# Attention with a relative-position bias and two expert layers on one core: the loads of two head pairs, the order of the attention sums and the split of x are moved

## Chip, cores and metric

One core of one Trainium2 chip. The time is device microseconds of one execution of the whole program; less is better. A kernel's time is the median of several executions.

## What is computed

Four batches of 8 heads, 576 tokens, head width 64. The attention output, reshaped to 2304 tokens of 512 values, goes through a layer with a rational activation and then through a layer with a maximum of three products:

```
scores = q @ k.T / 8
x      = log1p(|i - j|) / log1p(max(i, 1))
bias   = relu(x * w1 + b1) @ w2               # hidden width 32, one value per head
attn   = softmax(scores + bias)
x      = attn @ v                             # as [2304, 512]
h      = x @ w_in                             # [2304, 2048]
x      = (P(h) / Q(h)) @ w_out                # P cubic in h, Q quadratic in |h|
out    = max(x @ w1, x @ w2, x @ w3) @ w_out  # hidden width 768
```

## The kernel before

All in one instruction stream per engine, in the order in which the Python code writes it: the schedule of SP (which issues every DMA), TensorE, VectorE, GpSimd and ScalarE is the program order, so an instruction that waits holds up all that stands behind it on its engine.

**Bias stage.** The bias is the same for all batches. 36 groups (`bgroups`: five row tiles `t` of 128 queries, the last one of 64, in groups `g` of 16 rows) are made one after another. `bias_hidden` (L181, L183) writes four tiles `h` per group, one on ScalarE and three on VectorE as a rule, two groups ahead. `bias_out` multiplies them (L192), scales the result on ScalarE into `bo` (L198), and SP stores it to DRAM (L200). Three groups after a row tile is complete, `bias_load` (L207) reads it back for the head pairs 0 and 1; this waits on SP until the tile's stores have landed. In the same loop VectorE splits k and q of pairs 0 and 1 into high and low parts. A list `L0` says ahead of which group k and q (`load_kq`, L128 and L130) and v (`load_v`, L122) of pairs 2 and 3 of batch 0 are issued.

Most SBUF tiles (`h`, `bo`, bias tiles, k, q and v of batch 0, their splits, exponentials) share 35 buffers with the tag `slot`. A buffer is taken from those that are free; when none is, the first instruction that writes the new tile waits.

**Attention.** 80 units (`units`): one row tile of one head pair. In batch 0 the first two pairs go row tile by row tile (10 units), where the sums are handled by unit (`own`). All other pairs go in two groups: row tiles 0 and 1 (a two-unit group), then 2, 3 and 4 (a three-unit group). `attn_tick(n)` walks a list of steps, `A2`; unit n has its scores (`sc`, L241) and, on VectorE, the addition of the bias with the running minimum (`r0`, `r1`, L267), then the exponentials on ScalarE (`e0`, `e1`, L273). Unit n-1 has its sums guarded on GpSimd (`na`, L298), and at the end of its group `sums_turn` (`n`) takes reciprocals (L313), transposes them and SP writes them to DRAM (L323); `sums_load` (L333) reads them back, broadcast, into `att`, two units later. Unit n-2 is transposed on TensorE (`T`, L369, L375) into PSUM banks (four of the tag `bank`), which `v0` and `v1` copy out. When a group is through, `attn_v` (`av`, L420) multiplies by v, in one piece for two units and in pieces for three; then `st` runs `attn_store` (L426): VectorE multiplies the product by the returned reciprocals into `xs`, and SP stores that to `x_d` a unit later (L428).

In `attn_tick`, `loads_at` and `splits_at` say at which unit k and q of a later pair are loaded and at which unit GpSimd starts to split them (the first such step is L141). A pair whose load was issued already is skipped there. For pair 3 of batch 0 these are units 8 and 11.

**Turn to the FFN.** Eight units before the end (72) the first block of x is read back (`load_x`, L560). In each of the last four units `split_x` makes one quarter: ScalarE copies it (L567), GpSimd subtracts (L568), VectorE for the last quarter. Then the FFN runs: `ph` and `y` (L576), with the rational function on ScalarE and VectorE (L607 to L623) and its split `gs` (L633, L634) in between. The first steps of the FFN are mixed with the last `attn_tick` calls, from unit 80 on.

Of the kernel before, what the change touches and what calls it, by code (L numbers as in the profile page):

```python
# [26 lines left out]
HID = 32  # L27
TOFF = 572
TW = 1148
KN = {'RL': 2, 'NSG': 4, 'RX': 2, 'AVL': 2, 'NSLOT': 35, 'NRAW': 3, 'NRAWX': 2, 'NATT': 4, 'HB': 0, 'NE': 'd', 'FP': 2, 'BL': 4, 'T4': 0, 'LSP': 1, 'KX': 4, 'HT': 'ss', 'EVP': 'da', 'TTP': 'dda', 'NXS': 4, 'EARLY': 4, 'NM0': 0, 'MAN': 3, 'MANF': 3, 'HA': 2, 'H0': [34, 35], 'L0': [(14, 'k2'), (18, 'v2'), (24, 'k3')], 'B4': 2, 'H2': [1, 2, 4, 6, 8, 10, 12, 14, 16], 'SP0': [3, 4], 'BW': 3, 'A2': ['na', 'sc', 'sq1', 'av', 'T', 'r0', 'r1', 'n', 'st', 'p1', 'p2', 'sq', 'e0', 'e1', 'v0', 'v1'], 'LL': 7, 'SL': 3, 'LL0': 9, 'SL0': 2, 'SQ': [1], 'CUT2': 1, 'CUT3': 4, 'WS': 14, 'WR': 41, 'EV': {None: 'da', 's': 'da', 'j': 'aa'}, 'WT': 64, 'XT': 8, 'XA': 3, 'XB': 8, 'F': ['g2a', 'g2d', 'h', 'g1a', 'w', 'g2p', 'g1d', 'g1p', 'y', 'x', 'g3'], 'LOW': 0, 'LOM': 3, 'LOI': 2, 'GHI': 'dve', 'GLO': 'dve', 'BED': 8, 'BE0': 16, 'NU1': 'pool', 'XE': ['act', 'pool'], 'RS': 3, 'PW': 1, 'WP': 10, 'NPK': 27, 'YSP': 'act', 'LAG': 2, 'EV1': 'dve', 'XSE': 'act', 'STQ': 'sp', 'PUQ': 'sp', 'NB0': 0, 'HP': 0, 'SB': 2, 'XLA': 3, 'XLB': 6, 'XSA': 11, 'YL': 4, 'MIX': [1, 2, 3], 'YN': [(6, 2), (6, 4), (6, 6), (7, 1), (7, 3), (7, 5), (8, 1), (8, 3), (8, 4), (8, 5)], 'WLOW': 1, 'YSN': {5: 2, 6: 2, 7: 1, 8: 1, 9: 1, 10: 1, 11: 1, 12: 1}, 'PLAN': [(2, 1, [0, 2, 3, 4, 5, 6, 7, 8]), (3, 1, [4, 6, 7, 8, 9, 10, 11, 12]), (4, 1, [8, 10, 11, 12, 13, 14, 15, 16]), (5, 2, [1, 3, 5, 6, 8, 10, 12, 14]), (6, 3, [0, 2, 3, 4, 5, 6, 7, 8]), (7, 3, [4, 6, 7, 8, 9, 10, 11, 12]), (8, 3, [8, 10, 11, 12, 13, 14, 15, 16]), (0, 4, [0, 2, 3, 4, 5, 6, 7, 8]), (1, 4, [6, 8, 9, 10, 11, 12, 13, 14])], 'WPN': {13: 1, 14: 1, 15: 1}, 'OB': [1, 5]}  # L30
REBIAS = 2.0 ** -112
TOSIGN = -2.0 ** 32
QC = 1.0 + 1e-6
# [4 lines left out]
def tile_attention_moe(  # L38
# [7 lines left out]
    pe, act, dve, pool, sp = nc.tensor, nc.scalar, nc.vector, nc.gpsimd, nc.sync  # L46
# [17 lines left out]
    def big(name, shape, dt=F32):  # L64
        return sb.tile(shape, dt, tag="big", name=name, bufs=2)
# [7 lines left out]
    def f32(ap):  # L73
        return ap.bitcast(F32)
# [22 lines left out]
    A0, A1, A2, A3 = (par[:, i:i + 1] for i in range(4))  # L97
# [177 lines left out]
    def own(b, p):  # L275
        return b == 0 and p < KN["FP"]
# [286 lines left out]
    def split_x(tag, blk, kc):  # L563
        n = blocks[blk][1]
        rt = xr[tag, blk, kc // 2]
        t = slot(f"{tag}s{blk}_{kc}", [P, 2, n], F32R)
        act.copy(t[:, 0], rt[:, kc % 2])  # L567
        (dve if blk == 0 and kc == 3 else pool).tensor_tensor(t[:, 1], rt[:, kc % 2], f32(t[:, 0]), ALU.subtract)  # L568
        xt[tag, blk, kc] = t
# [351 lines left out]
    NU = len(units)  # L921
# [167 lines left out]
    def attn_tick(n):  # L1089
        if len(r_load) >= KN["RL"]:  # L1090
            for g in r_load.pop(0):
                sums_load(*g)
        for t, p in bloads_at.get(n, []):
            if (t, p) not in bias:
                bias_load(t, p)
        u0 = units[n] if n < NU else None
        u1 = units[n - 1] if 1 <= n <= NU else None
        u2 = units[n - KN["LAG"]] if KN["LAG"] <= n < NU + KN["LAG"] else None
        ev = []
        kind = early_kind(n)  # L1100
        evp, ttp = KN["EV"][kind] if n < KN["WT"] else (KN["EVP"][n % len(KN["EVP"])], KN["TTP"][n % len(KN["TTP"])])
        for step in KN["A2"]:
            if step == "sc" and u0:
                if u0[2] == u0[1][0]:
                    at_tiles(u0[0], u0[1], u0[3])
                    sums_begin(u0[0], tuple(u0[1]), u0[3])
                scores(u0[0], u0[2], u0[3])
            elif step in ("r0", "r1") and u0:
                reduce_min(u0[0], u0[2], u0[3], int(step[1]))
            elif step in ("e0", "e1") and u0 and (step == "e0" or u0[2] < 4):  # L1110
                expo(u0[0], u0[2], u0[3], int(step[1]))
            elif step == "st":
                while stq:
                    attn_store(*stq.pop(0))
            elif step == "T" and u2:
                ev = transposes(u2[0], u2[2], u2[3], n >= NU)
            elif step == "na" and u1:
                sum_guard(*u1)
            elif step == "n" and u1:
                sums_turn(*u1)  # L1120
                tail_copy(u1[0], u1[2], u1[3])
            elif step == "v0" and u2:
                act.copy(*ev[0])
            elif step == "v1" and u2:
                for e_ in ev[1:len(ev) - 1]:
                    evac(evp, e_)
                evac(ttp, ev[-1])
            elif step == "p1":
                early_pop(kind)
            elif step == "av":  # L1130
                if avq and avq[0][0] <= n:
                    _, av, js = avq.pop(0)
                    attn_v(*av, js)
                    if 4 in js:
                        stq.append(av)
                if u2 and u2[2] == u2[1][-1]:
                    av = (u2[0], u2[1], u2[3])
                    cuts = {1: (5,), 2: (3, 2), 3: (2, 2, 1), 4: (4, 0, 1), 5: (5,)}
                    cut = {1: (5,), 2: cuts[KN["CUT2"]], 3: cuts[KN["CUT3"]]}[len(u2[1])]
                    avq.extend((n + KN["AVL"], av, range(sum(cut[:k]), sum(cut[:k + 1]))) for k in range(len(cut)))  # L1140
            elif step == "sq1":
                for bp in splits_at.get(n, []):
                    sqq.extend(split_kq(*bp))
                if sqq:
                    sqq.pop(0)()
            elif step == "sq":
                for _ in range(KN["SQ"][n % len(KN["SQ"])]):
                    if sqq:
                        sqq.pop(0)()
        for b, p in loads_at.get(n, []):  # L1150
            if p % 2 == 0 and (b, p) not in vv:
                load_v(b, p)
            if (b, p) not in raws:
                load_kq(b, p)
        sums_flush()
        put_flush()
        WT, XT = KN["WT"], KN["XT"]
        if WT <= n < NU:
            k = n - WT
            weights_tick(int(k * KN["WP"] // 16 != (k - 1) * KN["WP"] // 16))  # L1160
        if n == NU - XT:
            load_x("x", x_d, 0, 0)
            load_x("x", x_d, 0, 1)
        if NU - 4 <= n < NU:
            split_x("x", 0, n - NU + 4)

    with ordered(KN["MAN"]):
        for n in range(KN["NM0"], NU):
# [1 line left out]
    n = NU  # L1170
# [108 lines left out]
```

## Time and profile before

| | us |
|---|---|
| median of 3 runs | 1022.03 |
| lowest, highest | 1020.81, 1023.33 |
| the profiled execution, own time | 1020.21 |
| its span in the trace | 1018.4 |
| TensorE busy in the span | 985.0 |
| VectorE busy | 748.2 |
| ScalarE busy | 638.1 |
| GpSimd busy | 485.4 |

PE is TensorE, DVE is VectorE, ACT is ScalarE, POOL is GpSimd; SPq is the instruction queue of SP. A row of the timeline is a run of equal instructions; the brackets at its end tell the idle time of its engine before it and what ended it. In a row of waits the first names are the instruction that waited, the ones behind the arrow what it waited for.

### The profile page before, as it was taken

The page shows a single profiled execution, that of the slowest core. Times are in us where ns is not written, and L with a number is a line of the kernel's source. Part 1 is how long each engine was busy: PE and PEld are TensorE (multiplying, and loading weights), DVE is VectorE, ACT ScalarE, POOL GpSimd, SP SyncE. Part 2 cuts the span into 40 slices and gives each one's busy share as a digit, 9 for nine tenths or more (in the row PEclk, how much of TensorE's full clock was granted, in tenths as well). Part 3 has the DMA queues.
Part 4 walks back from the last instruction along what each step waited for, and adds up shares of the span by engine and source line. Part 5 has one row for each costly group of instructions (what it writes and reads, how often), then busy time and mean ns, then how long its engine had stood idle before and what let it go on. Part 6 is the DMA issues. An engine that isn't in the chain of part 4 may idle for free. (4 is left out here: it accounts for less than half of the span.)

```text
span 1018.4 us, 17426 instructions
## 1 busy us (share of the span) xinstructions
PE 985.0 (97%) x6012; PEld 816.1 (80%) x6012; DVE 748.2 (73%) x1461; ACT 638.1 (63%) x1294; POOL 485.4 (48%) x579
## 2 busy tenths in 40 slices
PE   6789999999999999999999999999999999999998
PEld 2259777777877688788899888787899999999997
DVE  8876778687786999788788988788676455555544
ACT  8876778777788888778788778778631121131111
POOL 4015656667683445345635356469532641361111
PEclk9989999999999999999999999999999999999999
DMA  6987667676563532123233232412597467645701
GB/s 248 331 287 243 232 214 240 211 256 209 200 214 121 169 106 75 52 93 114 83 145 115 83 134 93 172 46 93 186 358 251 160 203 269 227 153 203 254 32 62
DMA packets 74360, 176.69 MB, mean 174 GB/s; under 512 B 8864, under 2 KB 30112, under 8 KB 74272
## 3 DMA queue, kind: packets, MB, share of 16 engines
q1 hardware_dynamic: 74272, 175.58, 50.3%
q8 instruction: 47, 0.77, 0.3%
q14 instruction: 41, 0.34, 0.1%
HBM read 128.95 MB, written 46.60 MB: 172 GB/s over the span
## 5 line engine op out<-in xcount | busy, mean ns | idle before, releaser
L576 PE MATMUL y<-gs,wwo 128*128 128x512 f32 (+1 forms) x940 | 213.8, 373 | 3.5 <-POOL gs L634 3.2
L576 PE MATMUL ph<-xs,wwi 128*128 128x512 f32 (+1 forms) x930 | 206.5, 370 | 1.9 <-DVE xs L568 0.9
L576 PEld LDWEIGHTS y<-gs,wwo 128*128 128x128 f32 x940 | 164.2, 188 | 39.8 <-POOL gs L634 6.5
L856 PE MATMUL pr<-yo,ws 128*128 128x384 f32 x875 | 190.9, 336 | 2.4 <-DVE m L845 2.4
L576 PEld LDWEIGHTS ph<-xs,wwi 128*128 128x128 f32 x930 | 162.4, 188 | 35.3 <-POOL xs L568 1.7
L634 POOL TENSOR_TENSOR gs<-gring,gs 128x512 fp32r<-128x512 f32 (+1 forms) x77 | 91.4, 1187 | 159.5 <-ACT gs L633 79.8
L856 PEld LDWEIGHTS pr<-yo,ws 128*128 128x128 f32 x875 | 155.2, 188 | 10.3 <-DVE m L845 6.0
L273 ACT ACTIVATE e<-e,st 128x576 f32<-128x576 f32 x144 | 110.8, 772 | 36.2 <-DVE st L267 31.2
L267 DVE CUSTOM_DVE_ANT_0 e<-s,bias 128x576 f32<-128x576 f32 x144 | 103.7, 752 | 20.3 <-PE s L252 11.9
L836 POOL TENSOR_TENSOR h<-m,h 128x384 fp32r<-128x384 f32 x36 | 36.7, 1019 | 161.6 <-ACT h L835 144.7
L607 ACT ACTIVATE s<-ph,keep 128x512 f32<-128x512 f32 (+1 forms) x80 | 49.6, 620 | 69.9 <-PE ph L576 69.4
L241 PE MATMUL s<-k,qs 128*128 128x288 f32 x512 | 85.9, 310 | 4.8 <-DVE st L267 3.0
L903 PE MATMUL o<-wmo,h 128*128 128x512 f32 x324 | 82.9, 393 | 0.0
L871 ACT COPY u<-pr 128x384 f32<-128x384 f32 x27 | 12.9, 478 | 106.8 <-PE pr L856 106.8
L369 PE MATMUL tp<-ident,e 128*128 128x128 f32 x564 | 78.2, 279 | 1.5 <-DVE xs L426 1.2
L369 PEld LDWEIGHTS tp<-ident,e 128*128 128x128 f32 x564 | 61.5, 141 | 20.9 <-DVE st L267 7.8
L241 PEld LDWEIGHTS s<-k,qs 128*128 128x128 f32 x512 | 71.4, 192 | 8.2 <-DVE st L267 5.0
L609 DVE SCALAR_TENSOR_TENSOR gring<-gring,keep,s 128x512 f32<-128x512 f32 (+1 forms) x77 | 53.0, 689 | 32.0 <-ACT gring L608 31.4
L420 PE MATMUL av<-at,v 128*64 128x320 f32 (+3 forms) x576 | 70.1, 385 | 0.0
L903 PEld LDWEIGHTS o<-wmo,h 128*128 128x128 f32 x324 | 60.1, 188 | 9.8
L621 DVE SCALAR_TENSOR_TENSOR gring<-gring,keep,s 128x512 f32<-128x512 f32 (+1 forms) x77 | 53.3, 692 | 16.6 <-ACT s L615 12.7
L192 PE MATMUL pb<-h,keep 128*32 128x288 f32 x576 | 48.0, 445 | 15.4 <-ACT bo L198 7.1
(171 smaller groups left out, 1828.3 us busy)
## 6 DMA issues: line engine op xcount, KB each, us to landing
ws<-ms_d SPq DMA_DIRECT2D x75, 512.0 KB
ms_d<-wring SPq DMA_DIRECT2D x21, 512.0 KB
bias_d<-bo SPq DMA_DIRECT2D x36, 288.0 KB
kr<-in_k SPq DMA_DIRECT2D x16, 576.0 KB
qr<-in_q SPq DMA_DIRECT2D x16, 576.0 KB
bias<-bias_d SPq DMA_DIRECT2D x16, 576.0 KB
nr<-in_m SPq DMA_DIRECT2D x18, 512.0 KB
wrwin<-in_wi SPq DMA_DIRECT2D x16, 512.0 KB
```

Source lines behind the costliest of these rows:

```text
L241: pe.matmul(pt[:, x, :HS], lhsT=qs[:, u, t * P:(t + 1) * P], rhs=ks[u][:, w, x * HS:(x + 1) * HS], start=w == 0, stop=w == 1,)
L267: dve.tensor_tensor_reduce(out=dst, in0=src, in1=bs, op0=ALU.add, op1=ALU.min, scale=-0.125, scalar=3.0e38, accum_out=st[:, u:u + 1],)
L273: act.activation(et[:, u], et[:, u], AF.Exp, bias=st[:, u:u + 1], scale=-1.0, accum_out=sums[b, t, p][u])
L369: pe.transpose(tp[:, j * P:(j + 1) * P], flat[:, 640 * u + j * P:640 * u + (j + 1) * P], ident)
L420: pe.matmul(po[r, :n], lhsT=l, rhs=m, start=j == 0, stop=j == 4, skip_group_check=True)
L576: pe.matmul(po, lhsT=wpart(key, a, k), rhs=rhs, start=first and i == 0, stop=last and i == 2)
L607: act.activation(s, ph, AF.Abs, scale=B0)
L609: dve.scalar_tensor_tensor(q, q, B1, s, ALU.mult, ALU.add)
L621: dve.scalar_tensor_tensor(u, u, A0, s, ALU.add, ALU.mult)
L634: pool.tensor_tensor(t[1], u, f32(t[0]), ALU.subtract)
L856: pe.matmul(pt, lhsT=w[:, a, ch * P:ch * P + P], rhs=ys[c][ch], start=ch == 0 and i == 0, stop=ch == 1 and i == 2,)
L903: pe.matmul(po, lhsT=h[:, a, (tt % 3) * P:(tt % 3 + 1) * P], rhs=mo_t[j][:, c], start=j == 0 and i == 0, stop=j == NF2 - 1 and i == 2,)
```

## The change

Only the table of constants, the list of steps and two conditions are touched.

- `L0`: k and q of pair 2 are issued ahead of group 3 (before: 14), v of pairs 2 and 3 ahead of group 6 (before: 18). k and q of pair 3 (before: group 24) are no longer issued in the bias stage, so `loads_at` issues them at unit 8 and GpSimd splits them from unit 11 on, as for any later pair.
- `A2`: the step `st` stands ahead of `n`.
- A two-unit group (not one of `own`) whose product is complete goes to `st_next`; `st` moves that list to `stq` after it has emptied `stq`, so its `attn_store` runs one unit later. Three-unit groups and `own` units are stored in the unit of their product as before.
- `A3` is the list of steps for the calls after unit 80: there the transposes and their copies stand ahead of `av`.
- `XS`: the four quarters of x are split in units 75 to 78 (before: 76 to 79).

```diff
 KN = {
...
+'XS': 5, 'A3': ['na', 'T', 'v0', 'v1', 'av', 'n', 'st'],
...
-'L0': [(14, 'k2'), (18, 'v2'), (24, 'k3')],
+'L0': [(3, 'k2'), (6, 'v2')],
...
-'A2': ['na', 'sc', 'sq1', 'av', 'T', 'r0', 'r1', 'n', 'st', 'p1', 'p2', 'sq', 'e0', 'e1', 'v0', 'v1'],
+'A2': ['na', 'sc', 'sq1', 'av', 'T', 'r0', 'r1', 'st', 'n', 'p1', 'p2', 'sq', 'e0', 'e1', 'v0', 'v1'],
...
-    avq, stq = [], []
+    avq, stq, st_next = [], [], []
...
-        for step in KN["A2"]:
+        for step in KN["A2"] if n <= NU else KN["A3"]:
...
             elif step == "st":
                 while stq:
                     attn_store(*stq.pop(0))
+                stq.extend(st_next)
+                st_next.clear()
...
                     if 4 in js:
-                        stq.append(av)
+                        (st_next if len(av[1]) == 2 and not own(av[0], av[2]) else stq).append(av)
...
-        if NU - 4 <= n < NU:
-            split_x("x", 0, n - NU + 4)
+        if NU - KN["XS"] <= n < NU - KN["XS"] + 4:
+            split_x("x", 0, n - NU + KN["XS"])
```

## Rows read from the trace of the kernel before

**Rows 1.** The page, busy tenths of TensorE in 40 slices of the span
```profile
PE   6789999999999999999999999999999999999998
```

**Rows 2.** Windows: PE, PEld, DVE, ACT, POOL busy us (count), granted clock, DMA share, GB/s
```profile
14.00:26.00 12.00, 9.18 (x128) 3.26 (x128) 11.87 (x25) 12.00 (x19) 4.40 (x10) 1.00 0.50 189
30.00:66.00 36.00, 29.41 (x357) 11.49 (x358) 28.55 (x65) 28.60 (x44) 0.00 (x0) 0.95 0.99 349
66.00:70.00 4.00, 3.85 (x17) 3.27 (x16) 3.04 (x9) 2.50 (x6) 0.25 (x1) 0.57 0.32 71
84.00:104.00 20.00, 20.00 (x200) 18.42 (x198) 13.41 (x40) 14.09 (x36) 8.76 (x21) 1.00 0.75 245
308.00:310.00 2.00, 2.00 (x20) 1.25 (x17) 1.84 (x6) 2.00 (x6) 0.00 (x0) 1.00 0.13 43
```

**Rows 3.** Waits from 46 to 66 us, VectorE and ScalarE: us, times, longest
```profile
DVE h L183 <- DMA bias_d<-bo: 3.5, 2, 2.6
...
ACT bo L198 <- DMA bias_d<-bo: 6.1, 2, 3.5
```

**Rows 4.** VectorE's timeline: start, us, line, instruction, count, idle time before
```profile
39.75 7.80 DVE L183 TENSOR_SCALAR h<-tab_sb,psi 128x576 f32<-128x576 f32 x18
...
50.14 7.66 DVE L183 TENSOR_SCALAR h<-tab_sb,psi 128x576 f32<-128x576 f32 x17 [2.58 <-DMA bias_d<-bo]
...
58.70 3.52 DVE L183 TENSOR_SCALAR h<-tab_sb,psi 128x576 f32<-128x576 f32 x8 [0.90 <-DMA bias_d<-bo]
...
66.05 0.76 DVE L267 CUSTOM_DVE_ANT_0 e<-s,bias 128x576 f32<-128x576 f32 x1 [3.83 <-PE s L241]
```

**Rows 5.** TensorE's timeline at the first scores
```profile
43.81 5.06 PE L192 MATMUL pb<-h,keep 128*32 128x288 f32 x64
...
65.22 1.50 PE L241 MATMUL s<-k,qs 128*128 128x288 f32 x8 [1.79 <-ACT bo L198]
...
66.88 3.94 PE L241 MATMUL s<-k,qs 128*128 128x288 f32 x16 [0.15 <-DVE st L267]
```

**Rows 6.** Waits of SP's queue from 20 to 66 us, the bias loads
```profile
SPq L207 <- DMA bias_d<-bo: 5.3, 4, 2.9
```

**Rows 7.** VectorE's waits from 65 to 345 us
```profile
DVE xs L426 <- DMA att<-r_d: 11.6, 4, 4.3
...
DVE sg L313 <- POOL sg L298: 4.4, 8, 1.0
```

**Rows 8.** TensorE's waits from 110 to 318 us
```profile
PE s L241 <- DVE st L267: 2.8, 5, 1.0
```

**Rows 9.** All engines' timeline at the longest wait for reciprocals
```profile
180.16 1.29 PE L241 MATMUL s<-k,qs 128*128 128x288 f32 x8
...
182.65 0.42 DVE L426 TENSOR_TENSOR xs<-av,att 128x256 f32<-128x256 f32 x1 [4.30 <-DMA att<-r_d]
...
183.13 0.65 PE L369 MATMUL tp<-ident,e 128*128 128x128 f32 x4 [1.24 <-DVE xs L426]
```

**Rows 10.** TensorE's timeline, transposes while a product is held
```profile
124.23 1.09 PE L369 MATMUL tp<-ident,e 128*128 128x128 f32 x8
```

**Rows 11.** TensorE's waits from 318 to 345 us
```profile
PE y L576 <- POOL gs L634: 1.2, 1, 1.2
...
PE ph L576 <- DVE xs L568: 0.9, 1, 0.9
...
PE ph L576 <- ACT xs L567: 0.3, 1, 0.3
```

**Rows 12.** VectorE's timeline at the turn to the FFN
```profile
320.91 0.29 DVE L392 COPY att<-tt 128x128 f32<-128x128 f32 x1 [1.01 <-PE tt L375]
...
323.89 1.35 DVE L568 TENSOR_TENSOR xs<-xr,xs 128x512 fp32r<-128x512 f32 x1 [0.34 <-ACT xs L567]
```

**Rows 13.** Timelines of SP (unit 8's bias load) and GpSimd (fourth pair's split)
```profile
85.63 0.37 SPq L207 DMA_DIRECT2D bias<-bias_d  x1
...
98.16 1.05 POOL L141 TENSOR_SCALAR qs<-qr 128x1024 fp32r<-128x1024 f32 x1
```

More of the change, by code (lines that the diff above doesn't have):

```diff
@@ L29 @@
 TW = 1148
-KN = {'RL': 2, 'NSG': 4, 'RX': 2, 'AVL': 2, 'NSLOT': 35, 'NRAW': 3, 'NRAWX': 2, 'NATT': 4, 'HB': 0, 'NE': 'd', 'FP': 2, 'BL': 4, 'T4': 0, 'LSP': 1, 'KX': 4, 'HT': 'ss', 'EVP': 'da', 'TTP': 'dda', 'NXS': 4, 'EARLY': 4, 'NM0': 0, 'MAN': 3, 'MANF': 3, 'HA': 2, 'H0': [34, 35], 'L0': [(14, 'k2'), (18, 'v2'), (24, 'k3')], 'B4': 2, 'H2': [1, 2, 4, 6, 8, 10, 12, 14, 16], 'SP0': [3, 4], 'BW': 3, 'A2': ['na', 'sc', 'sq1', 'av', 'T', 'r0', 'r1', 'n', 'st', 'p1', 'p2', 'sq', 'e0', 'e1', 'v0', 'v1'], 'LL': 7, 'SL': 3, 'LL0': 9, 'SL0': 2, 'SQ': [1], 'CUT2': 1, 'CUT3': 4, 'WS': 14, 'WR': 41, 'EV': {None: 'da', 's': 'da', 'j': 'aa'}, 'WT': 64, 'XT': 8, 'XA': 3, 'XB': 8, 'F': ['g2a', 'g2d', 'h', 'g1a', 'w', 'g2p', 'g1d', 'g1p', 'y', 'x', 'g3'], 'LOW': 0, 'LOM': 3, 'LOI': 2, 'GHI': 'dve', 'GLO': 'dve', 'BED': 8, 'BE0': 16, 'NU1': 'pool', 'XE': ['act', 'pool'], 'RS': 3, 'PW': 1, 'WP': 10, 'NPK': 27, 'YSP': 'act', 'LAG': 2, 'EV1': 'dve', 'XSE': 'act', 'STQ': 'sp', 'PUQ': 'sp', 'NB0': 0, 'HP': 0, 'SB': 2, 'XLA': 3, 'XLB': 6, 'XSA': 11, 'YL': 4, 'MIX': [1, 2, 3], 'YN': [(6, 2), (6, 4), (6, 6), (7, 1), (7, 3), (7, 5), (8, 1), (8, 3), (8, 4), (8, 5)], 'WLOW': 1, 'YSN': {5: 2, 6: 2, 7: 1, 8: 1, 9: 1, 10: 1, 11: 1, 12: 1}, 'PLAN': [(2, 1, [0, 2, 3, 4, 5, 6, 7, 8]), (3, 1, [4, 6, 7, 8, 9, 10, 11, 12]), (4, 1, [8, 10, 11, 12, 13, 14, 15, 16]), (5, 2, [1, 3, 5, 6, 8, 10, 12, 14]), (6, 3, [0, 2, 3, 4, 5, 6, 7, 8]), (7, 3, [4, 6, 7, 8, 9, 10, 11, 12]), (8, 3, [8, 10, 11, 12, 13, 14, 15, 16]), (0, 4, [0, 2, 3, 4, 5, 6, 7, 8]), (1, 4, [6, 8, 9, 10, 11, 12, 13, 14])], 'WPN': {13: 1, 14: 1, 15: 1}, 'OB': [1, 5]}
@@ new lines @@
+KN = {'XS': 5, 'A3': ['na', 'T', 'v0', 'v1', 'av', 'n', 'st'], 'RL': 2, 'NSG': 4, 'RX': 2, 'AVL': 2, 'NSLOT': 35, 'NRAW': 3, 'NRAWX': 2, 'NATT': 4, 'HB': 0, 'NE': 'd', 'FP': 2, 'BL': 4, 'T4': 0, 'LSP': 1, 'KX': 4, 'HT': 'ss', 'EVP': 'da', 'TTP': 'dda', 'NXS': 4, 'EARLY': 4, 'NM0': 0, 'MAN': 3, 'MANF': 3, 'HA': 2, 'H0': [34, 35], 'L0': [(3, 'k2'), (6, 'v2')], 'B4': 2, 'H2': [1, 2, 4, 6, 8, 10, 12, 14, 16], 'SP0': [3, 4], 'BW': 3, 'A2': ['na', 'sc', 'sq1', 'av', 'T', 'r0', 'r1', 'st', 'n', 'p1', 'p2', 'sq', 'e0', 'e1', 'v0', 'v1'], 'LL': 7, 'SL': 3, 'LL0': 9, 'SL0': 2, 'SQ': [1], 'CUT2': 1, 'CUT3': 4, 'WS': 14, 'WR': 41, 'EV': {None: 'da', 's': 'da', 'j': 'aa'}, 'WT': 64, 'XT': 8, 'XA': 3, 'XB': 8, 'F': ['g2a', 'g2d', 'h', 'g1a', 'w', 'g2p', 'g1d', 'g1p', 'y', 'x', 'g3'], 'LOW': 0, 'LOM': 3, 'LOI': 2, 'GHI': 'dve', 'GLO': 'dve', 'BED': 8, 'BE0': 16, 'NU1': 'pool', 'XE': ['act', 'pool'], 'RS': 3, 'PW': 1, 'WP': 10, 'NPK': 27, 'YSP': 'act', 'LAG': 2, 'EV1': 'dve', 'XSE': 'act', 'STQ': 'sp', 'PUQ': 'sp', 'NB0': 0, 'HP': 0, 'SB': 2, 'XLA': 3, 'XLB': 6, 'XSA': 11, 'YL': 4, 'MIX': [1, 2, 3], 'YN': [(6, 2), (6, 4), (6, 6), (7, 1), (7, 3), (7, 5), (8, 1), (8, 3), (8, 4), (8, 5)], 'WLOW': 1, 'YSN': {5: 2, 6: 2, 7: 1, 8: 1, 9: 1, 10: 1, 11: 1, 12: 1}, 'PLAN': [(2, 1, [0, 2, 3, 4, 5, 6, 7, 8]), (3, 1, [4, 6, 7, 8, 9, 10, 11, 12]), (4, 1, [8, 10, 11, 12, 13, 14, 15, 16]), (5, 2, [1, 3, 5, 6, 8, 10, 12, 14]), (6, 3, [0, 2, 3, 4, 5, 6, 7, 8]), (7, 3, [4, 6, 7, 8, 9, 10, 11, 12]), (8, 3, [8, 10, 11, 12, 13, 14, 15, 16]), (0, 4, [0, 2, 3, 4, 5, 6, 7, 8]), (1, 4, [6, 8, 9, 10, 11, 12, 13, 14])], 'WPN': {13: 1, 14: 1, 15: 1}, 'OB': [1, 5]}
```

## The prediction

> **What bounds the kernel now.** I read the slices of the span first. TensorE is busy nearly throughout; only the opening of the span lies under 9 tenths, and smaller holes hide in the nines [rows 1]. So a change here is worth the TensorE idle time that it takes away, and nothing else; I went through the idle time stage by stage, with the windows, then the waits of each engine in the stage, then the timeline at each hole.
>
> Bias stage (to about 65 us): from 30 to 66 us the DMA engines have a share of 0.99 at 349 GB/s, against 0.50 at 189 GB/s from 14 to 26 us [rows 2]. The waits of VectorE and ScalarE from 46 us on name the landing of bias stores, 3.5 and 6.1 us [rows 3]: `h` and `bo` tiles find no free slot until older stores have landed. Up to 47.5 us VectorE makes `h` without a hole; behind it come two holes of 2.58 and 0.90 us and one of 3.83 us that ends with the first scores [rows 4]. TensorE starts the first score at 65.22 us, 1.79 us idle before it [rows 5]. The stage is thus bound by VectorE until 47.5 us and by DMA from there.
>
> Attention (65 to about 321 us): TensorE is idle only behind VectorE. VectorE waits 11.6 us, four times and up to 4.3 us, in `attn_store` (L426), for the reciprocals that come back by DMA [rows 7]. TensorE pays 2.8 us for that in scores [rows 8] and 1.24 us in a transpose [rows 9], 4.0 us, and little else. Turn to the FFN: TensorE waits 0.3 + 0.9 us for the last quarter of x and 1.2 us for the first `gs` [rows 11].
>
> **Loads.** The third pair's k and q (2 x 128x1152x4 B = 1.18 MB) and v (0.59 MB) go from groups 14 and 18 to 3 and 6, that is from the full stretch into the half-empty one; the fourth pair's k and q (1.18 MB) leave the stage. The room between 14 and 26 us is 12 x 0.50 x 349 = 2.1 MB [rows 2], and 1.77 MB go in. The stretch behind loses 2.95 MB, or 8.4 us at 349 GB/s. What is late next is VectorE: 18 `h` in 7.80 us are 0.433 us each, and 25 (17 + 8) are left after 47.55 us, so it is done at 47.55 + 10.8 = 58.4 us if it never waits [rows 4]. TensorE needs 5.06/4 = 1.27 us for the last group [rows 5]; first score at 59.7 us, 5.5 us sooner. Does DMA keep up? From 26 to 58.4 us it owes 24 stores of 0.295 MB and six bias loads of 0.59 MB, 10.6 MB, 30.4 us at 349 GB/s in 32.4 us. Yes, but with 2 us in hand only; I take 5.2 us. Bounds: 5.5 above; below, 2.0, since three pairs of bias loads each hold the SP queue until their tile's stores have landed, 5.3 us in all [rows 6], and the DMA engines, which have a full queue during these waits now, may then run dry: 30.4 + 5.3 = 35.7 us, 3.3 us too long.
>
> The first scores run at a granted clock of 0.57 (between the levels of 1.2 and 2.4 GHz) between 66 and 70 us, after the idle time ahead of them [rows 2, 5]. The first 24 score matmuls take from 65.22 to 70.82 us, 5.6 us; at 1.29 us for 8 [rows 9] it would be 3.9, but VectorE and ScalarE need about their time too. With the idle time mostly gone I count 0.4 us (0 to 0.8).
>
> The fourth pair's k and q are now issued at unit 8, behind the bias load at 85.63 us. In the queue they stand ahead of a store of x, the bias loads for the units from 13 on and the first weight loads. They cost 1.18/0.349 = 3.4 us of DMA in a stretch (84 to 104 us) with a share of 0.75, 5 us of room in 20 [rows 2]. GpSimd takes them up at 98.16 us, 12 us after the issue [rows 13]; the bias loads behind have four units, over 12 us. So nothing, with cover of some 5 us; were it gone, at most the 3.4 us, once. The slots are no dearer: the same two tiles were held at that time before. The third pair's k, q and v hold three slots from group 3 on, in a stretch where a half-idle queue frees those of the stores quickly: nothing.
>
> **Sums of two-unit groups.** The multiply with the returned reciprocals, and the store of x behind it, come one unit later on VectorE (14 groups, 0.42 us each as before [rows 9], none added). What is queued behind the wait on VectorE is the copy of the transposed tile, and then the next `reduce_min`, for which ScalarE's exponentials and TensorE's scores wait; that is the way in which 4.30 us of wait on VectorE became 1.24 us on TensorE [rows 9], and more on the scores behind. A unit later the same multiply stands behind the reduces of the next unit. In the worst case the scores of that unit begin at 180.16 us, half of them (0.65 us) and two reduces of 0.76 us [rows 4] end at about 182.3, and the data are there at 182.65 us [rows 9]: 0.4 us are left of 4.3. The other three have more margin (their waits were under 3 us, less than a unit). So of the 4.0 us I take 3.6; bounds 1.5, if later reciprocals meet the same queue, and 4.0.
>
> What it holds longer: the PSUM bank of the product, so that the transposes of the next unit have three banks in place of four. The three-unit groups show what that costs: their product is held over two units, and in these the transposes run right behind the scores with no wait shown, as at 124.23 us, in the first unit after the one that opened the product [rows 10]. Nothing. The `att` tile is held a unit longer too, with four buffers for at most four groups. In the order of the steps the multiply now stands ahead of the reciprocal: up to 0.5 us later for reciprocals whose load is issued two units on, while VectorE now waits for GpSimd's guard there anyway (4.4 us, 8 times) [rows 7]. Nothing; without cover 0.5 us on a load that has units of time.
>
> **x a unit sooner.** ScalarE's copy and the subtraction of each quarter move one unit forward. The data are there: from 308 to 310 us, when the first copy will run, the DMA share is 0.13 [rows 2]. The last subtraction stands then ahead of the last unit's reduce, 1.35 us, in a place where VectorE has 1.01 us of idle time [rows 12]: it gives back about 0.4. The waits of 0.3 + 0.9 us go [rows 11], so 0.8 us net. In the last units transposes now also stand ahead of the product (step list A3), so ScalarE reaches the first rational function about 2 us earlier, and of the 1.2 us that TensorE waits for `gs` [rows 11] I take 0.5, as ScalarE's copy of it then waits for the second group of `ph`. Together 1.3 us; bounds 0.3 and 2.3.
>
> **A rule of the Trainium skill against it.** The rows: the bias loads' waits on landed stores are 5.3 us over the stage [rows 6], with the queue full. The Trainium skill (DMA: Bandwidth & Descriptors, "Anatomy of one DMA — SWDGE (gpsimd) path") puts some 2.0 us of fixed time on a DMA, mostly the receipt of the last write, which no row here shows alone. An estimate by that page would be 3 x 2.0 = 6.0 us of dry queue in place of 5.3, the first rival below at 0.7 us more.
>
> **Sum.** 5.2 + 0.4 + 3.6 + 1.3 = 10.5 us. The profiled execution took 1020.2 us: 1009.7. It ran 1.8 us under the median of 1022.0; from the median 1011.5 us. From the bounds: gains of 2.0 + 0 + 1.5 + 0.3 = 3.8 to 5.5 + 0.8 + 4.0 + 2.3 = 12.6 us, so 1009.4 to 1018.2.
>
> **Rivals.**
> First, the bias stage stays bound by DMA. The queue runs dry in the waits on stores, as above; the stage is then 35.7 - 32.4 = 3.3 us longer than VectorE wants. For it: 2 us in hand are little. Against it: of 35 slots some 18 are held by the table, the first operands and bias tiles and 8 by `h`, so nine stores may be in flight, 11 us of VectorE's work. 1011.5 + 3.3 = about 1015.
> Second, the wait for reciprocals only moves. The loads that delay them (k, q and v of the next pair) are issued at the same units and now arrive at a TensorE that is ahead; then half the 3.6 us come back, and the total gives about 1013.5, or 1015 with a late x. For it: 0.4 us of margin in the worst case. Against it: three of four have more.
> Third, slower: the longer-held PSUM bank. If the transposes one unit behind are given the bank of the product, not a free one, TensorE stands until the multiply is done, from about 0.4 us after the transposes begin to the end of the second reduce and the multiply: 1.0 us (two reduces of 0.76 us [rows 4] and the multiply, less the head start) in each of 14 groups, 14 us. It decides when only three banks are free and the next in turn is the held one. 1011.5 + 14 = 1025.5, above the median now. Against it stand [rows 10].
> Fourth, the change does not do what it says, where the loads moved to the early groups wait there for something: within 1 us of now for that part, 1016.5 in all.
>
> **How the numbers follow.** The forecast has a chance of 0.60; first rival 0.16, second 0.11, third 0.05, fourth 0.03; 0.05 for what I don't see, in equal parts within 0.3% of now and slower. A measurement of this kernel can tell 0.3%, 3.1 us, from no change. The range of 1007.5 to 1017 takes in the forecast, with 2 us for the runs' own scatter below, the first two rivals and most of the bounds. Faster: the forecast and the first, second and fourth rivals, 0.90, less 0.03 for their upper edge: 0.87. Same 0.06, slower 0.07.
>
> **What would show it.** First score near 60 us with no wait of `h` or `bo` on bias stores; if it stands near 63, the first rival. DMA share from 14 to 26 us near 0.9. L426's waits on `att` under 1 us each, and TensorE's 4.0 us of attention waits nearly gone; transposes waiting for L426 would be the third rival. `ph` with no wait on xs, `gs` under 0.8 us. GpSimd's split of the fourth pair without a wait on its load. The prediction is wrong if the gain at the first score is not still there at 1000 us, for TensorE has no other idle time in which to lose it.

## The result, and the profile after

| | before | after |
|---|---|---|
| median, us | 1021.79 (8 runs) | 1012.99 (8 runs) |
| lowest, highest | 1017.74, 1024.12 | 1007.72, 1016.53 |
| the profiled execution, own time | 1020.21 | 1015.52 |
| its span in the trace | 1018.4 | 1013.6 |
| TensorE busy in the span | 985.0 | 982.6 |

Ratio 0.9916, 95% interval 0.9888 to 0.9945: 8.8 us faster (5.6 to 11.4). The forecast was 1011.5 us, a gain of 10.5. The executions of the changed kernel lie 9 us apart; the profiled one is 2.5 us above their median and that of the kernel before 1.6 us below its own, so the two traces show a gain of 4.8 us and not 8.8.

**The bias stage.** Windows of the kernel after (busy us and count of PE, PEld, DVE, ACT, POOL, then granted clock, DMA share, GB/s), beside [rows 2]:

```profile
14.00:26.00 12.00, 9.18 (x128) 3.18 (x120) 11.88 (x24) 12.00 (x20) 4.25 (x10) 1.00 0.96 329
30.00:60.00 30.00, 25.83 (x336) 9.44 (x336) 28.19 (x65) 26.26 (x41) 0.00 (x0) 1.00 0.90 308
66.00:70.00 4.00, 4.00 (x34) 4.00 (x35) 3.81 (x12) 3.95 (x11) 2.22 (x6) 1.00 0.97 326
84.00:104.00 20.00, 20.00 (x196) 18.32 (x195) 12.84 (x36) 13.73 (x34) 10.84 (x20) 1.00 0.79 258
```

The loads have moved where the forecast put them: the share from 14 to 26 us is 0.96 in place of 0.50, and the full stretch behind it has some room. From 84 to 104 us TensorE stays full with the fourth pair's k and q in it.

Waits of the kernel after, VectorE and ScalarE from 46 to 66 us and SP's queue from 20 to 66 us (us in total, times, longest), beside [rows 3, 6]:

```profile
DVE h L183 <- DMA bias_d<-bo: 0.4, 1, 0.4
...
ACT bo L198 <- DMA bias_d<-bo: 3.7, 1, 3.7
...
SPq L207 <- DMA bias_d<-bo: 9.1, 10, 2.1
```

Timelines of the kernel after, VectorE and then TensorE, beside [rows 4, 5]:

```profile
35.73 12.53 DVE L183 TENSOR_SCALAR h<-tab_sb,psi 128x576 f32<-128x576 f32 x29
48.65 9.96 DVE L183 TENSOR_SCALAR h<-tab_sb,psi 128x576 f32<-128x576 f32 x23 [0.39 <-DMA bias_d<-bo]
...
60.54 1.18 PE L192 MATMUL pb<-h,keep 128*32 128x288 f32 x16 [2.43 <-ACT bo L198]
61.64 0.80 PE L241 MATMUL s<-k,qs 128*128 128x288 f32 x4
...
66.56 1.03 PE L369 MATMUL tp<-ident,e 128*128 128x128 f32 x8
```

VectorE has made its last `h` at 48.65 + 9.96 = 58.6 us; the forecast said 58.4. But ScalarE's `bo` behind it waits 3.7 us for a buffer, while SP waits for landed stores ten times, 9.1 us in all, and the first score starts at 61.64 us, not at 59.7.

**Attention.** VectorE's waits of the kernel after from 65 to 345 us, beside [rows 7], and TensorE's from 110 to 318 us, beside [rows 8]:

```profile
DVE sg L313 <- POOL sg L298: 5.9, 6, 1.8
DVE wnwin L471 <- DMA x_d<-xs: 3.1, 1, 3.1
...
DVE xs L426 <- DMA r_d<-sgt: 0.8, 1, 0.8
...
PE s L252 <- DVE st L267: 2.0, 2, 1.1
PE tp L369 <- ACT at L1125: 1.4, 3, 0.7
PE s L241 <- DVE st L267: 1.0, 2, 0.8
PE av L420 <- DVE xs L426: 0.2, 1, 0.2
PE tp L369 <- DVE at L392: 0.2, 1, 0.2
```

L426 no longer waits 11.6 us for `att` from `r_d`; all that is left is 0.8 us for the transfer ahead of it. TensorE, however, still waits 4.8 us in this stretch, where it waited 4.2 us: 2.8 in scores [rows 8], 1.24 in a transpose [rows 9] and 0.2 for a copy. The waits have other names: transposes wait for ScalarE's copy `at`, and VectorE is late for scores for reasons that the forecast had put at nothing or did not list.

**A ledger from the profiled executions.** Rows of the kernel before (the first transposes, the first `ph`, the first `y`), and the same of the kernel after (its first transposes are the row at 66.56 above):

```profile
70.66 1.04 PE L369 MATMUL tp<-ident,e 128*128 128x128 f32 x8
...
321.26 2.33 PE L576 MATMUL ph<-xs,wwi 128*128 128x512 f32 x9 [0.28 <-DVE att L392]
...
334.54 0.50 PE L576 MATMUL y<-gs,wwo 128*128 128x512 f32 x1
```

```profile
319.43 3.02 PE L576 MATMUL ph<-xs,wwi 128*128 128x512 f32 x12
...
330.83 0.40 PE L576 MATMUL y<-gs,wwo 128*128 128x512 f32 x1
```

| ahead of the kernel before at | us | change in the stretch |
|---|---|---|
| first score (65.22, 61.64) | 3.6 | +3.6 |
| first transposes (70.66, 66.56) | 4.1 | +0.5, the clock |
| first `ph` (321.26, 319.43) | 1.8 | -2.3 |
| first `y` (334.54, 330.83) | 3.7 | +1.9 |
| end of the span (1018.4, 1013.6) | 4.8 | +1.1 |

The two ends of the kernel gave what was forecast of them or somewhat less. Attention, from which 3.6 us were to come, took 2.3 us longer in this execution: TensorE is idle for 5.6 us between the first transposes and the first `ph`, in place of 4.6, and busy for 1.3 us more, with 1.7 us lost to a lower clock (last section).

### The profile page after: what moved, and what is told of

Read it like the earlier page. It is cut to its first block, busy times and chain, and to the rows that moved or that the text cites. A ratio compares the mean times of both kernels' runs of the same rounds, so it can differ in the third digit from the quotient of the medians.

```text
span 1013.6 us, 17416 instructions
## 1 busy us (share of the span) xinstructions
PE 982.6 (97%) x6012; PEld 815.6 (80%) x6012; DVE 749.6 (74%) x1461; ACT 637.5 (63%) x1294; POOL 485.7 (48%) x579
## 5 line engine op out<-in xcount | busy, mean ns | idle before, releaser
L192 PE MATMUL pb<-h,keep 128*32 128x288 f32 x576 | 45.9, 431 | 15.8 <-ACT bo L198 6.9
```

## The experiments

The kernels whose times stand under one heading ran on the same chip, beside the kernel before; the ratio is to that.

### The parts by themselves

**The loads alone.** The kernel before with the new table of loads.

```diff
-'L0': [(14, 'k2'), (18, 'v2'), (24, 'k3')],
+'L0': [(3, 'k2'), (6, 'v2')],
```

> The kernel before with the loads of the third and fourth pair moved, nothing else. The forecast's terms: first score near 60 us in place of 65.2, VectorE's waits for returned reciprocals as before (over 9 us), time 5 to 6 us under the kernel before. Rival, from the trace of the changed kernel, where the first score stands at 61.6 us behind a last wait of 3.7 us of ScalarE for a slot: first score at 61 to 62 us, gain 3 to 4 us. If the whole gain of 8.8 us is here, the other two parts are worth nothing.

1016.83 us against 1020.39; ratio 0.9964 (0.9946 to 0.9981), 3.6 us. TensorE's timeline at the first score, VectorE's waits from 65 to 345 us and TensorE's from 110 to 318 us of this kernel:

```profile
59.39 0.79 PE L241 MATMUL s<-k,qs 128*128 128x288 f32 x4
...
DVE xs L426 <- DMA att<-r_d: 7.9, 3, 2.8
...
PE s L241 <- DVE st L267: 4.6, 7, 1.2
PE s L252 <- DVE st L267: 0.6, 1, 0.6
```

The first score is 5.8 us sooner, the bound that VectorE sets (59.7 forecast). The first `ph` is only 3.5 us sooner (317.74 us). Of what is lost between, 1.2 us are waits of TensorE for VectorE (5.2 us in place of 4.0). TensorE is also busy for 1.6 us more from the first transposes to the first `ph` (247.6 us in place of 246.0), at a granted clock of 1.00; that I can put on no row.

**The later sums alone.** The kernel before with `st_next` and the new order in `A2`; the split of x and the loads as before; of the calls after unit 80 only the order of `st` and `n` changes.

```diff
-'A2': [..., 'r1', 'n', 'st', 'p1', ...],
+'A2': [..., 'r1', 'st', 'n', 'p1', ...],
...
+                stq.extend(st_next)
+                st_next.clear()
...
-                        stq.append(av)
+                        (st_next if len(av[1]) == 2 and not own(av[0], av[2]) else stq).append(av)
```

> The kernel before with the store of two-unit groups a unit later and the multiply ahead of the reciprocals, nothing else. Forecast: the 11.6 us of VectorE's waits in the multiply nearly gone, TensorE's 4.0 us of attention waits down to under 1 us, time 3 to 4 us under the kernel before. Rival: the wait moves to the reciprocals, which wait for the guard on GpSimd behind the split of k and q of the next pair; TensorE's attention waits stay at 3 us or more, time within 2 us of the kernel before.

1018.49 us; ratio 0.9983 (0.9966 to 1.0001), 1.9 us, not clear of no change. VectorE's waits for `att` are gone as in the whole change, but it waits 7.5 us for GpSimd's guard, in place of 4.4 [rows 7]. TensorE's waits of this kernel from 110 to 318 us:

```profile
PE tp L369 <- ACT at L1125: 3.4, 6, 0.7
PE s L241 <- DVE st L267: 1.6, 2, 1.2
PE s L252 <- DVE st L267: 0.5, 1, 0.5
```

5.5 us in place of 4.2: the forecast's under 1 us is missed, and the rival's sign (3 us or more) came. From the first transposes to the first `ph` this kernel takes 251.4 us in its trace, and the kernel before 250.6. The wait of transposes for ScalarE's copies is 3.4 us; it is 0.2 us in the kernel before, with the loads alone and with the split alone. It comes with this part of the change.

**The split of x alone.** The kernel before with `XS` 5 and the new list `A3`.

> The kernel before with the split of x a unit sooner and the new order of the last units, nothing else. Forecast: no wait of the first products of the FFN for x (1.2 us before) and the wait for the first gs down from 1.2 to about 0.7 us, but 0.4 us more ahead of them: 1.3 us under the kernel before. Rival: the last subtraction on VectorE gives most of it back, 0.5 us or nothing.

1018.90 us; ratio 0.9984 (0.9965 to 1.0003), 1.5 us, not clear of no change either. At the turn TensorE's waits are 0.8 us for `gs` and 0.8 us for VectorE's last minimum, in place of 0.3, 0.3, 0.9 and 1.2. VectorE's waits for `att` stand at 11.7 us, as before.

**The changed kernel once more.**

> The changed kernel once more, unaltered, for a second profile and beside the others on one chip. If the sum of the three parts holds, its gain is that of the three parts together, about 8 to 10 us. The trace of its first profile has 4.6 us of TensorE waits in attention in place of 4.0; if these are particular to that execution, this one has fewer.

1011.69 us; ratio 0.9917 (0.9892 to 0.9942), 8.7 us. The parts add up to 3.6 + 1.9 + 1.5 = 7.0 us, each with some 1.8 us either way; that the whole is more than its parts is thus not shown. The profiled execution (1015.04 us) again lies above the median, by 3.4 us. VectorE's and TensorE's timelines of this run, then the windows (TensorE alone: busy us and count, granted clock, DMA share, GB/s):

```profile
209.63 1.40 DVE L471 SCALAR_TENSOR_TENSOR wnwin<-wrwin 128x512 int32<-128x512 int32 x1 [4.10 <-DMA x_d<-xs]
...
211.75 2.01 PE L241 MATMUL s<-k,qs 128*128 128x288 f32 x8 [2.25 <-DVE st L267]
```

```profile
212.00:214.00 2.00, 2.00 (x10) 0.60 0.60 227
214.00:216.00 2.00, 2.00 (x10) 0.55 0.74 144
```

An FFN weight whose two halves VectorE joins (L471) waits 4.10 us, the next minimum is late for it, and TensorE stands 2.25 us; then its clock lies between 1.2 and 2.4 GHz for two windows, which is 2 x (1 - 0.60) + 2 x (1 - 0.55) = 1.7 us of work more. That is 4 us for one wait. The weight takes its buffer from the same ring of four, `xs`, as `attn_store`; a buffer is free when the store of x from it has landed. The store that is issued a unit later frees its buffer later.

### Three waits taken away one by one

All three are edits of the changed kernel.

**Bias loads two groups later.** A row tile is read back five groups after it is complete, so SP should find its stores landed.

```diff
-'BW': 3,
+'BW': 5,
```

> The changed kernel with the bias loads five groups behind the last group of their row tile in place of three, so that SP finds the stores landed and does not hold the queue. Theory (the last 3.7 us of the bias stage are SP's waits on landed stores, the first rival of the forecast): SP's waits at the bias loads fall from 9 us to under 2, ScalarE's wait of 3.7 us for a slot goes, first score at 59.4 to 59.9 in place of 61.6 us, time about 2 us under the changed kernel. Rival (the queue is simply too slow in this stretch): waits move from SP to the slots, first score stays at 61 to 62 us.

1012.94 us; ratio 0.9909 (0.9871 to 0.9946). SP's waits from 20 to 66 us and TensorE's first score:

```profile
SPq L207 <- DMA bias_d<-bo: 1.3, 1, 1.3
...
58.92 0.79 PE L241 MATMUL s<-k,qs 128*128 128x288 f32 x4
```

SP's wait on stores falls from 9.1 to 1.3 us, ScalarE's wait for a buffer is gone, and the first score is 2.7 us sooner than in the profile of the changed kernel. But three of the seven profiles with `BW` at 3 have their first score as early (59.39, 59.56 and 58.96 us) with 7.7 to 8.9 us of SP's waits. That the bias loads in SP's queue hold the stores back fits, and is not shown. The median does not show a gain.

**Five buffers for `xs`.** For room, one table goes to another tag and `NSG` from 4 to 3.

```diff
-'NSG': 4, ... 'NXS': 4,
+'NSG': 3, ... 'NXS': 5,
...
-    psi_sb = sb.tile([P, S // 4], F32, tag="psi", name="psi")
+    psi_sb = big("psi", [P, S // 4])
```

> The changed kernel with five buffers in the ring that x blocks and joined weights share, in place of four (room from the psi table, which moves to the buffers of the transposed tiles, and from one of four sum tiles). Theory: the store of two-unit groups a unit later holds its buffer longer, and VectorE waits 3.1 to 4.1 us at one joined weight (near 211 us) for a store of x to land, which costs TensorE 0.9 to 2.3 us of waiting and then some 2 us at the lower clock. With five buffers that wait is gone, the span is 2 to 4 us shorter. Rival: the wait there is another queue's, and only changes its name; same time as the changed kernel.

1012.12 us; ratio 0.9917 (0.9882 to 0.9953). L471 no longer waits on a store of x, the clock stays at 1.00 in every 10 us of attention, and the first `ph` is at 314.59 us. Transposes still wait 2.0 us (4 times) for ScalarE's copies, and products 1.1 us for a multiply. The 2 to 4 us that were expected do not show in the median.

**The multiply at the end of its own unit.** The multiply of a two-unit group stands behind the last steps of the unit in which its product is complete, not at `st` of the next.

```diff
+'A2': [..., 'v0', 'v1', 'st2'],
...
-                stq.extend(st_next)
-                st_next.clear()
+            elif step == "st2":
+                while st_next:
+                    attn_store(*st_next.pop(0))
```

> The changed kernel with the multiply of two-unit groups not a unit later but at the end of its own unit, behind the copies of the transposed tiles. It frees the PSUM bank and the x buffer before the next unit. Theory (a bank held a unit longer makes transposes wait for ScalarE's copy): the waits of transposes for ScalarE, 1.4 us in the first profile, go to 0.3; the wait at the joined weight near 211 us shrinks; but the returned reciprocals have about 1.5 us of grace in place of a unit, so up to 2 us of TensorE waits on VectorE come back. About the time of the changed kernel, up to 1.5 us less. Rival (the bank costs nothing): 1 to 3 us slower.

1012.58 us; ratio 0.9908 (0.9880 to 0.9936). The profiled execution took 1018.3 us, the longest of its ten. VectorE's waits from 65 to 345 us and TensorE's from 110 to 318 us:

```profile
DVE xs L426 <- DMA att<-r_d: 8.1, 5, 4.1
...
PE tp L369 <- DVE xs L426: 2.5, 2, 1.7
PE tp L369 <- ACT at L1126: 1.4, 4, 0.8
```

The end of the unit is not late enough: the reciprocals are waited for again, and twice transposes stand until the multiply has freed its bank, for 0.8 and 1.7 us, which is the third rival's mechanism. The waits for ScalarE's copies were to go to 0.3 us if the held bank made them; they are 1.4 us, as in the changed kernel. The medians can't tell the two kernels apart.

**The guard on VectorE.** For grouped sums the addition of 1e-9 moves from GpSimd to VectorE, right ahead of the reciprocal.

```diff
-        pool.tensor_scalar(r, r, 1e-9, 0.0, ALU.add, ALU.add)
+        if own(b, p):
+            pool.tensor_scalar(r, r, 1e-9, 0.0, ALU.add, ALU.add)
...
+        dve.tensor_scalar(r, r, 1e-9, 0.0, ALU.add, ALU.add)
```

> The changed kernel with the guard of the sums of grouped units on VectorE, right ahead of the reciprocal, in place of GpSimd, where it stands behind the split of k and q. Theory (the wait for returned reciprocals has in part become a wait for the guard): VectorE's wait of 4.2 to 4.8 us for the guard goes, 26 more instructions of some 0.2 us come, TensorE's waits in attention shrink by about 1 us; time 1 us under the changed kernel. Rival: VectorE waits for ScalarE's exponentials instead, same time.

1013.93 us; ratio 0.9926 (0.9900 to 0.9953). What it was to take away shows in the kernel after, GpSimd, VectorE, ScalarE and TensorE at 180 us:

```profile
178.58 1.42 POOL L150 TENSOR_TENSOR k<-kr,k 128x576 fp32r<-128x576 f32 x1
...
180.09 0.24 POOL L298 TENSOR_SCALAR sg<-sg 128x4 f32<-128x4 f32 x1
...
178.09 0.42 DVE L426 TENSOR_TENSOR xs<-av,att 128x256 f32<-128x256 f32 x1 [0.81 <-DMA r_d<-sgt]
180.36 0.18 DVE L313 RECIPROCAL sg<-sg 128x4 f32<-128x4 f32 x1 [1.85 <-POOL sg L298]
...
182.94 0.78 ACT L273 ACTIVATE e<-e,st 128x576 f32<-128x576 f32 x1 [2.81 <-DVE st L267]
...
178.57 2.37 PE L420 MATMUL av<-at,v 128*64 128x320 f32 x16 [0.20 <-DVE xs L426]
...
182.96 1.42 PE L252 MATMUL s<-k,qtail 128*128 128x288 f32 x10 [0.88 <-DVE st L267]
...
185.09 1.83 PE L369 MATMUL tp<-ident,e 128*128 128x128 f32 x8 [0.71 <-ACT at L1125]
```

The guard stands behind a pair's split on GpSimd; VectorE waits 1.85 us for it, ScalarE then 2.81 us for VectorE's minimum, and TensorE 0.88 us for that minimum and 0.71 us for ScalarE's copy. No product of a two-unit group is held at the time of the last wait: its multiply ran at 178.09 us, and the product that is open is that of a three-unit group, as in the kernel before. With the guard on VectorE the wait is gone, and so are these two holes; elsewhere transposes still wait 2.3 us (6 times) for copies. The median is none the better.

### Together, and two parts taken back

**The three edits together** (bias loads two groups later, five buffers, the guard on VectorE).

> The changed kernel with three of the steps tried singly, together: bias loads five groups behind, the ring of five, the guard on VectorE. Theory (each takes away its own wait): first score at 59 to 59.6 us, no wait of a joined weight for a store of x, none for the guard on GpSimd; TensorE's waits in attention from 4.6 to 3 us or less; time 3 to 5 us under the changed kernel, ratio to the kernel before 0.987 to 0.989. Rival (what one step frees, the next wait takes): the ratio of the changed kernel, 0.991 to 0.992.

1010.99 us (1010.07 to 1011.55); ratio 0.9900 (0.9885 to 0.9916), between what the theory and the rival gave. The first score is at 59.10 us, and the waits for the guard and for a store of x are gone. But TensorE waits 5.5 us from 110 to 318 us, where 3 us or less were expected: 1.8 us for copies, 1.2 us for a multiply, 1.0 us for GpSimd's split, a new name, and 1.5 us for VectorE's minimum. What one step frees, other waits take in part.

**The same, and the last quarter of x subtracted on GpSimd.**

```diff
-        (dve if blk == 0 and kc == 3 else pool).tensor_tensor(t[:, 1], ...)
+        pool.tensor_tensor(t[:, 1], ...)
```

> The kernel of the run before it with the last quarter of x subtracted on GpSimd in place of VectorE. Theory: the 1.53 us of VectorE ahead of the last reduce are the cause of TensorE's wait of 0.77 us ahead of the first products of the FFN; GpSimd is idle there for 2.2 us. The wait goes to under 0.2 us, the products wait for no quarter of x; 0.6 us less than the run before it, which the time alone can't show. Rival: the products then wait for GpSimd by as much.

1009.84 us (1009.26 to 1010.64); ratio 0.9892 (0.9876 to 0.9908), 11.0 us. GpSimd, VectorE and TensorE at the turn, the kernel after first (VectorE and TensorE):

```profile
317.08 1.53 DVE L568 TENSOR_TENSOR xs<-xr,xs 128x512 fp32r<-128x512 f32 x1 [0.15 <-ACT xs L567]
318.54 0.74 DVE L267 CUSTOM_DVE_ANT_0 e<-s,bias 128x576 f32<-128x576 f32 x1
...
319.35 0.33 PE L375 MATMUL tw<-ident,e 128*128 128x128 f32 x1 [0.77 <-DVE st L267]
```

```profile
312.60 0.75 DVE L267 CUSTOM_DVE_ANT_0 e<-s,bias 128x576 f32<-128x576 f32 x1
312.87 1.29 POOL L570 TENSOR_TENSOR xs<-xr,xs 128x512 fp32r<-128x512 f32 x1 [1.74 <-ACT xs L569]
...
314.17 0.27 PE L377 MATMUL tw<-ident,e 128*128 128x128 f32 x1
```

The minimum no longer stands behind the subtraction, and the hole of 0.77 us is gone. Of all kernels this has the lowest median. It is below the kernel before beyond doubt; its interval overlaps that of the changed kernel (0.9892 to 0.9942), so that it beats that one as well is likely and not shown.

**The old order of the steps.** The changed kernel with `n` ahead of `st` again; two-unit groups still go a unit later.

> The changed kernel with the reciprocals ahead of the multiply, as before the change; the multiply of two-unit groups stays a unit later. Theory (the held PSUM bank makes transposes wait for ScalarE's copies): TensorE's waits for these copies stay at 1 to 3 us, against 0.2 in every kernel without the later store. Rival (the swap is the cause): they go back to 0.2 us. Time that of the changed kernel within 2 us.

1011.16 us; ratio 0.9900 (0.9880 to 0.9921). TensorE's waits from 110 to 318 us:

```profile
PE av L420 <- DVE xs L426: 2.6, 4, 1.0
...
PE tp L369 <- ACT at L1125: 0.2, 1, 0.2
```

The order of the two steps is not where the gain is. The transposes' wait falls to 0.2 us, which is the rival's sign and not that of the held bank, and in its place products wait for the multiply, 2.6 us. Products and transposes take their PSUM tiles from the same four banks (the tag `bank`). The swap goes with a shift from one wait to the other, in one profile of either order; how, no run shows.

**The fourth pair's k and q in the bias stage again.** The changed kernel with `(24, 'k3')` back.

> The changed kernel with k and q of the fourth pair loaded ahead of group 24 again; k, q and v of the third pair stay early. It shows what taking 1.18 MB out of the stage is worth: by the sum of bytes the stretch behind 26 us has 11.8 MB, 33.7 us at 349 GB/s in 32.4 us, and with two more slots held. Theory: DMA ends the stage, first score at 63 to 64 us in place of 61.6, time 1 to 2.5 us over the changed kernel. Rival (the early loads alone are the gain): first score as in the changed kernel. In attention nothing differs.

1013.75 us; ratio 0.9934 (0.9908 to 0.9959). From 30 to 60 us the DMA share is back at 0.99 (350 GB/s), `h` waits 2.4 us and `bo` 3.1 us on stores, and the first score is at 62.12 us, sooner than the 63 to 64 us expected. The ratio is 1.8 us above that of the changed kernel, as expected, but the intervals overlap, so what these two loads alone are worth is not settled.

## Why the prediction was right, and where its steps were off

**The time.** 1011.5 was forecast, 1012.99 and 1011.69 were measured, inside the range, and both intervals lie clear of no change. The total came as forecast; how it is made up did not. Without the 3.6 us for the sums the forecast would have been 1015.1 us, inside the range as well, so that the range was kept says little for that term. In the traces the gain stands ahead of the first transposes and behind the first `ph`, and attention between them is in no profile more than 0.8 us shorter than the 250.6 us of the kernel before.

**Loads, 5.2 us: the mechanism right, the size somewhat large.** VectorE's end of the stage came within 0.2 us of its forecast, and with the loads alone the first score reached the forecast bound. Over the seven profiles with these loads and `BW` at 3 (after, loads alone, repeat, five buffers, multiply at the end, guard, old order) the first score is at 61.64, 59.39, 61.66, 59.56, 61.81, 60.90 and 58.96 us, 60.6 in the mean; with the old loads it is at 65.22, 64.64 and 64.38, 64.7 in the mean. So 4.2 us, not 5.2.

The seven fall into two sets. In three the first score is at 58.96 to 59.56 us and ScalarE's wait for a buffer 1.3 to 1.4 us; in four it is at 60.90 to 61.81 us and that wait 2.9 to 3.7 us. In the first set the DMA engines moved 378 to 400 GB/s from 54 to 58 us, in the second 245 to 285. The missing 1 us is thus of the first rival's kind, a stage that DMA ends; its mechanism is not shown, for SP's waits on stores are nearly as long in the early set (7.7 to 8.9 us) as in the late one (8.9 to 11.4 us). Reading the tiles back later takes SP's wait away, and all three profiles with `BW` at 5 are early (58.92 to 59.36 us). I had seen both sides ("2 us in hand are little") and gave the whole to the forecast, nothing of the 3.3 us to the rival. The 6.0 us that the prediction estimates by the Trainium skill rest on a section about DMAs that GpSimd issues; here SP issues them all, and no run shows the fixed time alone.

**The clock, 0.4 us: the size right, by luck.** From the first score to the first transposes 5.44 us became 4.92, 0.5 us. The first scores now stand at 61.64 to 66.56 us, and the granted clock from 60 to 66 us is 1.00, in place of 0.57 at their old place. But it does not hang on the loads: with the sums alone and the split alone, under the old loads, the first scores ran at 1.00 too and took 4.63 and 4.61 us; with the guard on VectorE, under the new loads, the clock fell to 0.50 and they took 5.70 us.

**The fourth pair's loads at unit 8, nothing: right.** GpSimd's first split and TensorE from 84 to 104 us show no wait for them. GpSimd waits longer for q of the two pairs behind (4.4 and 4.0 us, and before 2.2 us, once); no wait of TensorE names these loads.

**Sums, 3.6 us: the wait went as forecast, the gain did not.** This is the step that failed: that a wait taken off VectorE is 3.6 us on TensorE. VectorE's 11.6 us fell to almost nothing, also in the part alone, which measured 1.9 us (-0.1 to 3.5). From the first transposes to the first `ph` the profiles show 250.6 us before and 251.4 with the later sums; under the new loads 253.5 without them, 252.9 and 252.5 with them. Three things that I had priced at nothing, or not at all, stand in the place of the old wait:
- ScalarE's copies. Transposes wait for them 0.2 us without the later multiply (before, loads alone, split alone), 0.2 us with it under the old order of the steps, and 1.0 to 3.4 us with it in the nine other profiles. I first took this for the PSUM bank that the two-unit product holds longer, and the traces speak against it. Both longer waits of the kernel after (0.50 us at 120.02 us, 0.71 at 185.09), and five of the six with the sums alone, come while a three-unit product is open and no two-unit product is held. In both of the kernel after, VectorE has waited for the guard (1.06 and 1.85 us), ScalarE for VectorE's minimum (1.54 and 2.81 us), and the copy is late for that. The guard is not all of it, since copies are waited for with the guard on VectorE too (2.3 us), and with the old order VectorE waits 6.4 us for the guard and the transposes only 0.2. [rows 10], one row without a wait, could not price this. A run with a fifth bank was not made, and the cause stays open.
- The ring of `xs`. A store issued a unit later frees its buffer later, and a joined weight waited for it in the middle of VectorE's queue: 3.1 and 4.1 us in the two profiles of the changed kernel, 3.8 with the sums alone, none in the kernel before, none in the three profiles with five buffers, none with the multiply in its own unit. It cost up to 2.25 us of TensorE and, in that profile, 1.7 us of clock. This cause is shown, in the trace. I had followed the bank, `att` and the reciprocal that are held longer, and not the tile that the multiply writes.
- The guard. I called VectorE's waits for it harmless since they were there before (4.4 us). Once the reciprocals no longer set the pace, one of 1.85 us was the next thing late; TensorE's two holes behind it went when the guard was moved.

The second rival (the wait for reciprocals only moves) describes the sum of it, though not the cause: the wait moved to GpSimd's guard, ScalarE's copies and a ring, not to later reciprocals. The third rival's wait, transposes for a multiply, came twice where the multiply stood at the end of its unit (2.5 us), and never in the changed kernel. It stood already in the kernel before: the 1.24 us of [rows 9] end with the multiply (182.65 + 0.42 us), so they are the product's bank, and not the copy behind the multiply as the prediction reads them. Products that wait for a multiply are a kin of it: 2.6 us in the old order of steps, 0.2 us in the kernel after.

**Split of x, 1.3 us: right.** From `ph` to `y` 13.28 us became 11.40: 1.9 us won; the hole ahead of `ph` is 0.77 us in place of 0.28, so 0.5 us go off, about the 0.4 forecast. 1.4 us net; the part alone measured 1.5 us (-0.3 to 3.6).

**The last sentence of the prediction was wrong.** It held that a gain at the first score can't be lost, for lack of other idle time. With the loads alone 6.4 us of lead at the first transposes (64.28 us against 70.66) were 3.5 us at the first `ph`. So a stage without idle time in one trace had some in another; that its engines meet the DMA queue and GpSimd at other times would explain it, and is not shown.

**What stays open.** The single edits each remove a wait in the trace and leave the median where it was; the three together have a median 0.7 to 2.0 us lower than the changed kernel's two. The nine executions with the three edits (four of them with the last quarter of x on GpSimd too) lie between 1009.26 and 1011.55 us, where the 18 of the changed kernel lie between 1007.72 and 1018.43; the waits may thus be what spreads them. Whether they are was not tested. And 1.1 us of the ledger, behind the first `y`, has 0.4 us of a row (the projections' wait for VectorE, 2.4 us before and 2.0 after), and no more; with the loads alone and the sums alone, which change nothing there, this stretch is 0.4 and 0.8 us shorter than before as well.

## What to carry to other kernels

When an instruction is moved later to escape a wait, list every buffer that it reads or writes and every ring that these belong to (PSUM bank, output tile, store), and ask who takes the next one; "the wait is gone" is worth TensorE's idle time only if none of these is short. One row without a wait does not price a shared resource; count its waits over all places where the pattern stands, and before a buffer is named as the cause, look at which tile holds it when the wait comes. And where executions of a kernel lie 9 us apart, read the trace for causes and the medians for sizes: three edits here that took waits of 1.9 to 3.7 us out of the trace could not be seen in the median by themselves.

## What was not expected of the hardware

The clock fell after holes that had done nothing before. In the kernel after, at 184 us (windows of TensorE: busy us and count, granted clock, DMA share, GB/s):

```profile
184.00:186.00 2.00, 1.29 (x9) 0.82 0.77 242
186.00:188.00 2.00, 2.00 (x11) 0.50 0.83 281
188.00:190.00 2.00, 2.00 (x13) 0.83 0.68 115
```

Two holes of 0.88 and 0.71 us, 2.1 us apart, were followed by a stretch at 0.50, the level of 1.2 GHz, in which eight score matmuls took 2.17 us and not 1.30. In the kernel before, TensorE was as idle there (1.24 us at 183.13 [rows 9] and 0.60 us at 184.49), and its clock stayed at 1.00 from 180 to 192 us. The same pair of holes, as far apart, left the clock at 1.00 in two other kernels (0.83 and 0.70 us with the bias loads later, 0.96 and 0.71 us with `k3` back). Ahead of the first scores a hole of 2.43 us left it at 1.00 in the kernel after, and one of 2.20 us was followed by 0.50 with the guard on VectorE. So the length of a hole alone did not tell in these traces what it costs: 2 x (0.18 + 0.50 + 0.17) = 1.7 us on top of 1.6 us of holes here, nothing there. The Trainium skill (TensorE: Matmul & The Clock Gate, "Part 1: The HAM clock gate (the "warmup" mystery)") says that this gate grants one of two levels and nothing between them. The 0.82 and 0.83 beside the 0.50 agree with it if their windows hold some of each.
